# Small group's sums in 128x32 strips behind the low-rank sums, and two edits in the first slot

## The chip, the cores and the metric

The kernel runs on one core of a Trainium2 chip. The metric is the device time of one execution in microseconds (us). Before the change it was 979.74 us, the median of three runs (979.51 to 979.88).

The engines' short names are PE (TensorE; PEld is its weight load), DVE (VectorE), ACT (ScalarE), POOL (GpSimd) and SP (SyncE, which here issues nearly all DMAs).

## The reference

There are eight batches of 3136 rows and 256 columns; z has 64 columns, the low rank is 32, the hidden width 1024. Attention without softmax comes first, then a mixer over rows of low rank, then a two-layer mixer over columns:

```python
scores = (1 / S) * z @ z.T
attn = maximum(scores, 0) ** 2
x = u * (attn @ v)                       # B x 3136 x 256
h = x.T @ U @ V                          # U: 3136 x 32, V: 32 x 3136
u2 = x + h.T
out = u2 + maximum(u2 @ w_ch1, 0) @ w_ch2
```

## The kernel before

**Tiles.** 3136 rows are 24 tiles of 128 and one of 64. They are worked on in seven groups per batch: six of 512 rows (g = 0 to 5) and the *small group* (g = 6, 64 rows). Time goes in 56 *slots*, t = 7 b + g. A slot of g < 6 runs the attention stream of its group, `av_stream`: 48 steps in each of two "ways" of two 64x128 matmuls each, on the upper and the lower half of the rows, that run at the same time and write to different PSUM banks. `pair` (L174 to L184) issues two such matmuls. Seven slots later comes the group's low-rank part (`u2_unit`), and eight slots later its two-layer mixer (`ch1_part`, `ch2_stream`).

**Order.** Everything is emitted in a hand-written order into each engine's queue, which runs strictly in that order. In `emit` a slot has a list of light units (the streams) and queues of items (place, need, turn, function): an item is issued ahead of the light unit whose number is its place, if `need` of the four PSUM tiles are free by the planner's books, or else up to 14 units later. An item of need 0 is never put off. An item with `turn` first puts a no-op on POOL that waits for PE (`post`), changes the way of the attention stream and, in the first slot, takes one entry of `spare`: two casts of a piece of v on POOL (`cast_v`, L1310). The planner's clock counts one unit for a pair of matmuls of 256 columns. `hold(due, f)` runs `f` when that clock has reached `due`, or earlier when something that is emitted needs it. `book` keeps what each of ACT, DVE and SP is thought to be busy until.

**Scores.** A score pair (512 columns in two banks) must be rectified and squared. `rectify` with `whole` in the first slot chooses by the books among three ways: `both` (ACT rectifies, DVE squares later), `act` (two passes of ACT) and `dve` (`one_pass`: DVE rectifies and squares at once). The list `ways` gives the first choices by hand; with it empty, the way that ends first is taken. The first slot has fifteen such calls: one ahead of it, then at places 4, 16, 24, 30, 40, 46, 50, 56, 64, 68 (the pair called "last"), 72, 78, 84 and 88.

**First slot.** `cast_tail` (place 58) casts z's and v's last 64 rows, `z_turn` at place 62 transposes z's on PE (L331). The casts of v's six pieces are on POOL: one piece before the slot and one with each of the turns at places 4, 12, 24, 40 and 56.

**Sums of the small group.** Its attention output (64 rows) is `av_small`: 52 matmuls in the 64x64 form, four at a time, which end as four partial sums in two banks and two halves of the partitions. `four_sums` adds them: ACT copies the upper half (L759), DVE adds the lower half (L761), DVE adds the two banks (L763). `ch2_small` does the same for its second mixer layer (16 matmuls, L1145). For batches 2 to 7 both run one after the other in slot g = 0 at place 72: `ch2_small` of batch b - 2 and `av_small` of batch b. For batches 0 and 1 `av_small` runs alone, and for batches 6 and 7 `ch2_small` runs alone at the end.

**Low-rank sums.** `t1_all` (x.T @ U, L825 and L835) runs in 128x32 *strips*: all 128 rows, four column strips with different tiles of the sum, four matmuls at a time. It runs in slot g = 0 of the batch after (place 8), and for the last batch in the last slot. Its upper half is added to the lower by ACT (L847), DVE (L848) and a DVE copy (L849); `u2_unit` (L910) of the same slot needs it. The sixth piece of v of batch b (the last 512 full rows) is cast in slot g = 6 of the batch before or at the start of slot g = 0, by the function `cast`, which takes ACT or DVE, whichever is free first by the books (L204, L206).

Of the kernel before, what the change touches and what calls it, by code (L numbers as in the profile page):

```python
# [18 lines left out]
def kernel(  # L19
# [11 lines left out]
    nc = tc.nc  # L31
# [73 lines left out]
    ways = ["both", "dve"]  # L105
# [198 lines left out]
    def load_u(b, g):  # L304
        g0, gw = groups[g]
        if gw >= P:
            t = pool.tile([P, GT, D], FP32, name="u_sb", bufs=2)
            nc.sync.dma_start(
                out=t[:, : gw // P, :],
                in_=rows_of(u[b])[:, g0 // P : (g0 + gw) // P, :],  # L310
            )
        else:
            t = pool.tile([P, 3, D], FP32, name="u_small", bufs=1)
            nc.sync.dma_start(out=t[:gw, 0, :], in_=u[b, g0 : g0 + gw, :])
        queued(gw)
        u_sbs[b, g] = t
# [49 lines left out]
    def rectify(dst, src, b, part=1, whole=False):  # L366
# [24 lines left out]
        return book("act", ready, 8.7 if part == 1 else 5.3), None  # L391
# [335 lines left out]
    def av_small(b, g):  # L727
        k, ps = take_ps()
        rows = groups[g][1]
        xs[b, g] = pool.tile([P, 1, D], BF16, name="x_small")  # L730
        nc.vector.memset(xs[b, g][rows:, 0, :], 0.0)
        for jt in range(NQ + 1):
            while (b, jt) not in v_cast:
                run_held(min(h[0] for h in held))
        for jt in range(NT + 1):
            c = jt % 2
            part = slice(0, D) if jt < NF else slice(c * D // 2, (c + 1) * D // 2)
            at = min(jt, NF)
            for h in range(2):
                nc.tensor.matmul(  # L740
                    out=ps[c * hp : c * hp + rows, h, part],
                    lhsT=smalls[b][h * hp : (h + 1) * hp, place_of(at), :],
                    rhs=v_bfs[b][h * hp : (h + 1) * hp, at, part],
                    start=(jt < 2),
                    stop=(jt >= NF),
                    tile_position=(h * hp, c * hp),
                )
        pe(NT / 2 + 2)
        u1 = u_sbs[b, g]
        four_sums(k, ps, u1[:rows, 1:3, :])  # L750
        nc.vector.tensor_tensor(
            out=xs[b, g][:rows, 0, :], in0=u1[:rows, 1, :], in1=u1[:rows, 0, :], op=ALU.mult
        )
        book("dve", clock[0] + 3, 3)

    def four_sums(k, ps, t):

        rows = t.shape[0]
        nc.scalar.copy(out=t, in_=ps[hp : hp + rows, :, :D])  # L759
        ready = book("act", clock[0] + 3, 5)  # L760
        nc.vector.tensor_tensor(out=t, in0=ps[:rows, :, :D], in1=t, op=ALU.add)  # L761
        ps_free[k] = book("dve", ready + 1, 6)
        nc.vector.tensor_tensor(out=t[:, 0, :], in0=t[:, 0, :], in1=t[:, 1, :], op=ALU.add)  # L763
        book("dve", ready, 4)
# [53 lines left out]
    def t1_all(b):  # L818
# [26 lines left out]
        up = pool.tile([P, D], FP32, name="t1_up", bufs=1)  # L845
# [15 lines left out]
    def u2_unit(b, g, turn=True):  # L861
# [145 lines left out]
    def small_relu(b, g):  # L1007

        return flat_of(relus[b, g][0])[:, : NH * groups[g][1]]

    def ch1_small(b, g, way, box):
# [4 lines left out]
        if way == 0:  # L1016
            relus[b, g] = [take_block()]
# [106 lines left out]
    def ch2_out(b, g, acc):  # L1124

        for e in relus.pop((b, g)):
            give_block(e)
# [10 lines left out]

    def ch2_small(b, g):
        k, ps = take_ps()  # L1140
        rows = groups[g][1]
        for kt in range(NH):
            c = kt % 2
            for h in range(2):
                nc.tensor.matmul(  # L1145
                    out=ps[c * hp : c * hp + rows, h, :D],
                    lhsT=small_relu(b, g)[h * hp : (h + 1) * hp, kt * rows : (kt + 1) * rows],
                    rhs=w2_bf[h * hp : (h + 1) * hp, kt, :],
                    start=(kt < 2),
                    stop=(kt >= NH - 2),  # L1150
                    tile_position=(h * hp, c * hp),
                )
        pe(NH / 2 + 2)
        sums = u2s[b, g][:rows, 1:3, :]
        four_sums(k, ps, sums)
        ch2_out(b, g, sums[:, 0:1, :])
        book("dve", clock[0] + 3, 3)
# [156 lines left out]
    def cast_tail():  # L1314
        t0, n, entry, raw = zraw[2]
        for c in range(2):
            on_dve(out=z_bfs[0][:, NF, c, :], in_=raw[:, 2 * GT * dqk : n * dqk])
        v_tail(0, n, raw, on_dve)
        book("dve", clock[0], 5)
# [75 lines left out]
    for t in range(n_items):  # L1395
# [11 lines left out]
        if t > NG and g_now == NQ and b_next < B:  # L1407
            hold(clock[0] + 60 + 70, lambda b=b_next: load_u(b, NQ))
# [58 lines left out]
        elif av:  # L1467
# [20 lines left out]
        else:  # L1488

            small = (lambda: None) if early(*att) else (lambda: av_small(*att))  # L1490
            order = mine[:1] + [small] + mine[1:]
            if mix:
# [6 lines left out]
                else:  # L1499
                    order = up + [small, c0, c1, d0, d1, c2, c3, lambda: t1_all(att[0]), d2, d3]  # L1500
# [82 lines left out]
```

## Time and profile before

| what | us |
|---|---|
| median of three runs | 979.74 |
| the profiled execution | 979.08 |
| its span (first to last instruction) | 977.30 |
| PE busy | 969.4 |
| DVE busy | 633.7 |
| ACT busy | 480.0 |
| POOL busy | 15.7 |
| ps<-attn_small sums, L740, 8 batches, busy | 13.7 |
| ps<-relu sums, L1145, 8 batches, busy | 5.0 |
| ps<-x sums, L825 and L835, 8 batches, busy | 8.3 |
| last matmul's end | 973.02 |

The times of the prediction are microseconds from the span's start. A timeline line has start, duration, engine, line and operation, the tiles written and read, the array form of a matmul (64*128 and so on), and how often it is repeated; in brackets stand the engine's idle time ahead of it and what ended that. Matmuls overlap: one of 256 columns takes 0.27 us from its start to its end, so what counts is from start to start.

### The profile page before, as it was taken

To read this page: it belongs to the slowest core of one execution; us is meant where nothing else is said; L and a number is where in the kernel's file an instruction comes from. 1 tells how busy PE (TensorE), PEld (TensorE's weight loads), DVE (VectorE), ACT (ScalarE), POOL (GpSimd) and SP (SyncE) were. 2 spreads that over 40 slices of the span, in tenths; PEclk is the share of its full clock that TensorE was granted. 3 is DMA by queue.
4 is the path that set the end of the run, shared out by engine and by line. 5 is a ranking of instruction groups with operands and counts; after the bars stand their busy time and mean duration, and the time that the engine had idled before them with its cause. 6 is when DMAs were issued, how large, how long until landed. Compare 5 with 4: busy or idle time off the path is not lost.

```text
span 977.3 us, 35450 instructions
## 1 busy us (share of the span) xinstructions
PE 969.4 (99%) x16211; PEld 774.7 (79%) x16211; DVE 633.7 (65%) x815; ACT 480.0 (49%) x562; POOL 15.7 (2%) x25
## 2 busy tenths in 40 slices
PE   8999999999999999999999999999999999999998
PEld 6798777887778777787778877788777888778765
DVE  6887865668556775557756577556765667653363
ACT  8877732457334563345543365433653346531353
POOL 4200000000000000000000000000000000000000
PEclk9999999999999999999999999999999999999999
DMA  9999899989988799997999679996999968974142
GB/s 271 193 202 223 207 208 209 201 192 182 198 211 161 182 197 189 210 147 186 182 222 195 139 185 198 213 185 131 198 213 202 192 133 183 179 137 101 50 116 98
DMA packets 372549, 176.37 MB, mean 180 GB/s; under 512 B 347312, under 2 KB 350896, under 8 KB 372400
## 3 DMA queue, kind: packets, MB, share of 16 engines
q1 hardware_dynamic: 372256, 173.98, 87.2%
q8 instruction: 126, 2.06, 0.9%
q14 instruction: 23, 0.19, 0.1%
q10 hardware_dynamic: 144, 0.13, 0.0%
HBM read 62.56 MB, written 25.69 MB: 90 GB/s over the span
## 4 chain that ended last, share of the span: by engine, by line
PE 98%; DVE 1%; ACT 0%; issue 0%; DVEq 0%
PE ps L184 95%; PE ps L740 1%; PE ps L825 1%; PE ps L1145 0%; ACT blk L390 0%; DVE blk L364 0%; PE ps L1349 0%; PE ps L331 0%; DVE blk L553 0%; DVE blk L397 0%; DVE x_bf L775 0%; ACT last_sb L390 0%; DVE blk L1113 0%; PE ps L542 0%; DVE blk L761 0%
## 5 line engine op out<-in xcount | busy, mean ns | idle before, releaser
L184 PEld LDWEIGHTS <-blk 64*128 64x128 bf16 x12288 | 610.9, 94 | 152.6 <-POOLq L174 8.9
L184 PE MATMUL ps<-v_bf,blk 64*128 64x256 bf16 x9216 | 610.2, 269 | 1.0 <-DVE blk L364 0.8
L390 ACT ACTIVATE blk<-ps 128x1024 bf16<-128x1024 f32 (+1 forms) x335 | 313.8, 969 | 344.0 <-PE ps L184 339.0
L364 DVE TENSOR_TENSOR blk<-blk 128x1024 bf16<-128x1024 bf16 x350 | 222.3, 658 | 46.2 <-ACT blk L390 45.6
L184 PE MATMUL ps<-u2T,w_bf 64*128 64x512 bf16 (+1 forms) x1792 | 226.2, 349 | 0.0
L1002 DVE TENSOR_SCALAR blk<-ps 128x1024 bf16<-128x1024 f32 x111 | 135.9, 1224 | 103.7 <-PE ps L184 102.8
L184 PE MATMUL ps<-w_bf,blk 64*128 64x256 bf16 x3072 | 189.8, 269 | 0.0
L1005 ACT ACTIVATE blk<-ps 128x1024 bf16<-128x1024 f32 x81 | 82.2, 1022 | 123.9 <-PE ps L184 120.1
L184 PE MATMUL ps<-zzT 64*128 64x512 bf16 (+2 forms) x898 | 128.1, 326 | 0.6 <-ACT zzT L340 0.6
L184 PEld LDWEIGHTS <-w_bf 64*128 64x128 bf16 x1792 | 82.2, 94 | 27.9 <-POOLq L174 5.2
L775 DVE TENSOR_TENSOR x_bf<-ps,u_sb 128x1024 bf16<-128x1024 f32 x48 | 58.7, 1222 | 68.4 <-PE ps L184 68.4
L910 DVE TENSOR_TENSOR out_sb<-ps,x_bf 128x1024 f32<-128x1024 f32 x42 | 51.4, 1223 | 57.4 <-PE ps L184 57.4
L1131 DVE TENSOR_TENSOR out_sb<-ps,out_sb 128x1024 f32<-128x1024 f32 x42 | 51.4, 1224 | 19.2 <-PE ps L184 19.2
L184 PEld LDWEIGHTS <-zzT 64*128 64x128 bf16 x898 | 41.6, 94 | 6.3 <-ACT zzT L340 0.8
L206 DVE CAST v_bf<-stage 128x1024 bf16<-128x1024 f32 (+1 forms) x35 | 21.5, 615 | 0.0
L386 DVE TENSOR_SCALAR blk<-ps 128x1024 bf16<-128x1024 f32 x14 | 17.1, 1223 | 6.5 <-PE ps L184 5.8
L184 PE MATMUL ps<-t_sb,V_bf 64*128 64x256 bf16 (+1 forms) x208 | 20.3, 265 | 0.0
L204 ACT CAST x_bf<-out_sb 128x1024 bf16<-128x1024 f32 x19 | 19.7, 1037 | 0.0
L184 PE MATMUL ps<-v_bf,last_sb 64*128 64x256 bf16 x192 | 18.5, 269 | 0.0
L1131 DVE TENSOR_TENSOR blk<-ps,blk 128x1024 f32<-128x1024 f32 x5 | 6.1, 1225 | 11.9 <-PE ps L184 11.8
L204 ACT CAST v_bf<-stage 128x1024 bf16<-128x1024 f32 x13 | 13.5, 1040 | 0.0
L626 ACT ACTIVATE attn_small<-ps 128x512 bf16<-128x512 f32 (+1 forms) x32 | 13.1, 499 | 0.0
(86 smaller groups left out, 239.1 us busy)
## 6 DMA issues: line engine op xcount, KB each, us to landing
u_sb<-in_u_dram SPq DMA_DIRECT2D x48, 512.0 KB, 5.1
stage<-in_v_dram SPq DMA_DIRECT2D x42, 512.0 KB, 6.4
out_dram<-out_sb SPq DMA_DIRECT2D x42, 512.0 KB, 3.1
stage<-in_z_dram SPq DMA_DIRECT2D x7, 512.0 KB, 6.3
blk<-in_v_dram SPq DMA_DIRECT2D x5, 512.0 KB, 6.1
out_dram<-blk SPq DMA_DIRECT2D x5, 512.0 KB, 2.8
blk<-blk SPq DMA_TRANSPOSE x156, 5.1
blk<-in_moe_w_ch_dram SPq DMA_DIRECT2D x4, 512.0 KB, 5.5
```

The source lines that it names most:

```text
L184: ins = nc.tensor.matmul(**args)
L204: nc.scalar.copy(out=out, in_=in_)
L206: nc.vector.tensor_copy(out=out, in_=in_)
L364: nc.vector.tensor_tensor(out=a, in0=a, in1=a, op=ALU.mult)
L386: nc.vector.tensor_scalar(out=dst, in0=src, scalar1=scale, scalar2=0.0, op0=ALU.mult, op1=ALU.max)
L390: nc.scalar.activation(out=dst, in_=src, func=AF.Relu, scale=scale)
L626: nc.scalar.activation(out=dst[:, jj], in_=src[:, jj], func=AF.Relu, scale=scale)
L775: nc.vector.tensor_tensor(out=xs[b, g][:rows, :n, :], in0=four(box["ps"])[:rows, :n, :], in1=u_sbs[b, g][:rows, :n, :], op=ALU.mult,)
L910: nc.vector.tensor_tensor(out=o, in0=four(ps), in1=x, op=ALU.add)
L1002: nc.vector.tensor_single_scalar(out=r, in_=ps[:, :, :gw], scalar=0.0, op=ALU.max)
L1005: nc.scalar.activation(out=r, in_=ps[:, :, :gw], func=AF.Relu)
L1131: nc.vector.tensor_tensor(out=o, in0=acc, in1=o, op=ALU.add)
```

## The change

1. `av_small` and `ch2_small` become `small_sums`, whose matmuls are 128x32 strips (`in_strips`): per tile of the sum two matmuls of 128 rows by 32 columns instead of two of 64 by 64, and even and odd tiles of the sum in different halves of the partitions. So two partial sums are left instead of four; ch2's go to bank 0 and the attention's to bank 1 of one PSUM tile, one ACT copy and one DVE add serve both.
2. It is called right behind `t1_all` (`both_sums`) at place 8 of slot g = 0 for batches 2 to 7, with a need of two PSUM tiles. The ch2 part there is that of batch b - 3 (from batch 3 on), one batch later than before; batch 5's comes in the last slot behind `t1_all`. In the last phase batch 7's moves from place 9 to place 5. u2's place becomes 12 instead of 22 there.
3. The buffers follow: the small group's u2 in `out_small`, its relu in `relu_small` (no block of the shared store), t1's scratch and the sums' in `out_sb`; the small group's u is loaded 10 instead of 130 units into slot g = 6.
4. In the first slot `ways` gives ten choices: the sixth and the tenth call are `dve` too. In the books a rectify on ACT counts 9.3 instead of 8.7 in the first two slots.
5. `cast_tail` casts on POOL, and books nothing on DVE.

```diff
-    ways = ["both", "dve"]
+    ways = ["both", "dve", "both", "both", "both", "dve", "both", "both", "both", "dve"]
...
-            ends = {"dve": dve + DVE, "act": act + 19, "both": max(act + 8.7, dve) + 7.5}
+            ends = {"dve": dve + DVE, "act": act + 19, "both": max(act + 9.3, dve) + 7.5}
...
-        return book("act", ready, 8.7 if part == 1 else 5.3), None
+        return book("act", ready, 5.3 if part != 1 else 9.3 if slot[0] < 2 else 8.7), None
...
+    def in_strips(ps, bank, lhs, rhs, n, odd):
+        m = P // NREP
+        for i in range(n):
+            whole = i < n - 1 or not odd
+            for c in range(NREP) if not whole else (i % 2 * 2, i % 2 * 2 + 1):
+                w = c % 2
+                part = slice(0, D) if whole else slice(c // 2 * D // 2, (c // 2 + 1) * D // 2)
+                nc.tensor.matmul(
+                    out=ps[c * m : (c + 1) * m, bank, part],
+                    lhsT=lhs(i, slice(w * m, (w + 1) * m)),
+                    rhs=rhs(i)[:, part],
+                    start=(i < 2),
+                    stop=(i >= n - 2 if not odd else not whole),
+                    tile_position=(0, c * m),
+                )
+        pe(n / 2 + 1)
+
+    def small_sums(second, first, into=None):
+        k, ps = take_ps()
+        rows = groups[NQ][1]
+        if second is not None:
+            in_strips(
+                ps, 0,
+                lambda i, w: small_relu(second, NQ)[:, i * rows : (i + 1) * rows][:, w],
+                lambda i: w2_bf[:, i, :],
+                NH, False,
+            )
+        if first is not None:
+            b = first
+            xs[b, NQ] = pool.tile([P, 1, D], BF16, name="x_small")
+            nc.vector.memset(xs[b, NQ][rows:, 0, :], 0.0)
+            for jt in range(NQ + 1):
+                while (b, jt) not in v_cast:
+                    run_held(min(h[0] for h in held))
+            in_strips(
+                ps, 1,
+                lambda i, w: smalls[b][:, place_of(i), w],
+                lambda i: v_bfs[b][:, i, :],
+                NT, True,
+            )
+        at, end = 0 if second is not None else 1, 2 if first is not None else 1
+        n = end - at
+        t = (into or sums_tile())[:rows]
+        nc.scalar.copy(out=t[:, at:end], in_=ps[hp : hp + rows, at:end, :D])
+        ready = book("act", clock[0] + 3, 1 + 2 * n)
+        nc.vector.tensor_tensor(out=t[:, at:end], in0=ps[:rows, at:end, :D], in1=t[:, at:end], op=ALU.add)
+        ps_free[k] = book("dve", ready + 1, 1 + 2.5 * n)
+        if first is not None:
+            nc.vector.tensor_tensor(
+                out=xs[first, NQ][:rows, 0, :], in0=t[:, 1, :], in1=u_sbs[first, NQ][:rows, 0, :], op=ALU.mult
+            )
+            book("dve", clock[0] + 3, 3)
+        if second is not None:
+            ch2_out(second, NQ, t[:, 0:1, :])
+            book("dve", clock[0] + 3, 3)
...
+    def sums_tile():
+        return pool.tile([P, GT, D], FP32, name="out_sb", bufs=3)
+
+    def both_sums(b, second, first):
+        t = sums_tile()
+        t1_all(b, t)
+        small_sums(second, first, t)
...
+        elif n < GT:
+            o = pool.tile([P, 1, D], FP32, name="out_small", bufs=2)
...
-            relus[b, g] = [take_block()]
+            relus[b, g] = pool.tile([P, NH * gw], BF16, name="relu_small", bufs=1)
...
-            on_dve(out=z_bfs[0][:, NF, c, :], in_=raw[:, 2 * GT * dqk : n * dqk])
-        v_tail(0, n, raw, on_dve)
-        book("dve", clock[0], 5)
+            on_pool(out=z_bfs[0][:, NF, c, :], in_=raw[:, 2 * GT * dqk : n * dqk])
+        v_tail(0, n, raw, on_pool)
...
-            hold(clock[0] + 60 + 70, lambda b=b_next: load_u(b, NQ))
+            hold(clock[0] + 10, lambda b=b_next: load_u(b, NQ))
...
-                qc.append((64, 2, False, lambda: av_small(1, NQ)))
-            if fin:
-                qc.append((72, 2, False, lambda: (ch2_small(*fin), av_small(att[0], NQ))))
+                qc.append((64, 2, False, lambda: small_sums(None, 1)))
...
-                    order = up + [small, c0, c1, d0, d1, c2, c3, lambda: t1_all(att[0]), d2, d3]
+                    order = up + [small, c0, c1, d0, d1, c2, c3, lambda: both_sums(att[0], B - 3, None), d2, d3]
...
-                qm.append((8, 1, False, lambda: t1_all(u2i[0])))
-            qm.append((22 if u2i[1] == 0 else 40, 1, False, lambda: u2_unit(*u2i)))
+                sums = t > NG
+                b = att[0]
+                qm.append(
+                    (8, 2 if sums else 1, False,
+                        lambda: both_sums(b - 1, b - 3 if b > 2 else None, b) if sums else t1_all(b - 1))
+                )
+            qm.append((40 if u2i[1] else 12 if sums else 22, 1, False, lambda: u2_unit(*u2i)))
...
-                qm.append((9, 1, False, lambda b=B - 2 if k == 1 else B - 1: ch2_small(b, NQ)))
+                qm.append((9 if k == 1 else 5, 1, False, lambda b=B - 2 if k == 1 else B - 1: small_sums(b, None)))
```

More of the change, by code (lines that the diff above doesn't have):

```diff
@@ L312, in load_u @@
         else:
-            t = pool.tile([P, 3, D], FP32, name="u_small", bufs=1)
+            t = pool.tile([P, 1, D], FP32, name="u_small", bufs=1)
             nc.sync.dma_start(out=t[:gw, 0, :], in_=u[b, g0 : g0 + gw, :])
@@ L723, in av_stream @@
         return Ways(2 * NF, 1, step, box)
-    def av_small(b, g):
-        k, ps = take_ps()
[L729 to L764, printed above, removed]
+    def in_strips(ps, bank, lhs, rhs, n, odd):
[14 more added lines that the diff above has]
+        pe(n / 2 + 1)
@@ L843, in t1_all @@
         pe(7)
-        up = pool.tile([P, D], FP32, name="t1_up", bufs=1)
+        up = (into or sums_tile())[:, 2, :]
         t1 = pool.tile([P, D], BF16, name="t1_sb")
@@ L1136, in ch2_out @@
             give_block(o_blocks.pop((b, g)))
[L1139 to L1157, printed above, removed]
     def emit(light, queues, av=None, slack=14, hurry=14):
```

26 lines of the change are left out of this document (21 added, 5 removed).

## The prediction

> **What bounds the kernel now.** I read the page first: busy times, then the chain that ended last.
>
> ```profile
> PE 969.4 (99%) x16211; PEld 774.7 (79%) x16211; DVE 633.7 (65%) x815; ACT 480.0 (49%) x562; POOL 15.7 (2%) x25
> ...
> PE 98%; DVE 1%; ACT 0%; issue 0%; DVEq 0%
> ```
>
> TensorE is the chain. Since a busy PE need not be at its peak, I took the busy time by stretches (engine order PE, PEld, DVE, ACT, POOL):
>
> ```profile
> 4.80:27.00 22.20, 19.56 (x278) 12.63 (x279) 18.29 (x27) 19.38 (x23) 9.90 (x14) 1.00 1.03 288
> 27.00:930.00 903.00, 903.00 (x15260) 729.42 (x15256) 589.50 (x757) 437.78 (x514) 5.14 (x5) 1.00 0.91 182
> ```
>
> From 27 us on PE never idles, at a granted clock of 1.00. Only in the first slot are ScalarE (19.4 of 22.2 us) and VectorE (18.3) nearly full, and PE waits. So the change can act in three places: work or pauses of PE itself, the first 27 us, and the end. A steady pair of 64x128 matmuls over 256 columns starts every 0.109 us (eight pairs from 333.53 to 334.41 below); a four of 128x32 or 64x64 matmuls also takes 0.11 (24 of L825 in 0.66 us). Then I looked, in the PE timeline of one batch, at what surrounds the two groups that the change joins:
>
> ```profile
> 331.86 0.93 PE L184 MATMUL ps<-v_bf,blk 64*128 64x256 bf16 x14
> 332.73 0.84 PE L825 MATMUL ps<-x_bf,U_bf 128*32 128x256 bf16 x24
> 333.39 0.20 PE L835 MATMUL ps<-x_small,U_bf 128*32 128x64 bf16 x4
> 333.53 1.05 PE L184 MATMUL ps<-v_bf,blk 64*128 64x256 bf16 x16
> 334.41 0.49 PE L184 MATMUL ps<-zzT 64*128 64x256 bf16 x4
> ...
> 341.41 1.36 PE L184 MATMUL ps<-v_bf,blk 64*128 64x256 bf16 x22
> 342.70 0.63 PE L1145 MATMUL ps<-w_bf,blk 64*64 64x256 bf16 x16
> 343.17 1.54 PE L740 MATMUL ps<-v_bf,attn_small 64*64 64x256 bf16 x52
> 344.63 1.05 PE L184 MATMUL ps<-v_bf,blk 64*128 64x256 bf16 x16
> ```
>
> 331.86 to 334.41 is 2.55 us. Fifteen pairs (1.64), six fours (0.65) and a four of 64 columns (0.03) make 2.32: a visit to the 128x32 form loses 0.23 us going in and out. 341.41 to 344.63 is 3.22; eleven pairs (1.20), sixteen fours (1.74) and one of 128 columns (0.06) make 3.00: 0.22, and 0.01 more in the pair behind. From 342.70 to 343.17, where L1145 gives way to L740 in one form, four fours take 0.47, hardly over 0.44. So the loss belongs to a change of the array's form.
>
> **Part 1, the merge.** The matmuls stay: per batch 16 for ch2 and 52 for the attention sums, four at a time before and after, 0.11 us a four in either form. What goes are visits. Before: 8 of t1, one each of the attention sums alone (batches 0 and 1), 6 joint ones, and ch2 alone for batches 6 and 7 at the end: 18. After: attention 0, t1 0, attention 1, then t1+sums for slots 14, 21, 28, 35, 42 and 49, t1+ch2 in the last slot, and the two at the end: 12. Six fewer by 0.23: **-1.4 us**.
>
> The ACT copy (0.58) and VectorE add (0.68) that the two sums now share, and the second adds (0.42 each) that strips don't need, hang on engines with slack; I cost their loss at nothing. Loading u_small 120 clock units sooner puts one 64 KB transfer (5.5 us to land) some 9 us ahead of its use, and moves it on SP's queue ahead of the small turn (326.79), which is needed by 337. The small out-DMA moves to the first third of the slot; what then stands behind it on SP is the turn of x_bf (339.15), at worst 1 us later, and its reader runs after 344. Again nothing.
>
> It adds one wait. The attention sums, formerly at 343.17, now follow t1 and so need the last piece of v, whose cast is put on ACT just behind t1's copy:
>
> ```profile
> 333.65 0.37 ACT L847 COPY t_up<-ps 64x256 f32<-64x256 f32 x1 [0.55 <-PE ps L835]
> 333.92 1.04 ACT L204 CAST v_bf<-stage 128x1024 bf16<-128x1024 f32 x1
> 334.99 1.51 ACT L390 ACTIVATE blk<-ps 128x512 bf16<-128x512 f32 x2
> ```
>
> The cast ends 1.57 us after L835 starts (334.96 - 333.39), and with 0.06 for the signal PE may read it at 1.63. PE arrives at that piece (the eleventh four) after 0.03 + 0.44 for ch2 + 1.09 = 1.56: it waits 0.07, in five batches; in slot 14 there is no ch2 ahead and it waits 0.5. Together **+0.8**, between 0 (a free VectorE takes the cast) and 2 (0.3 each of ACT lateness). All queued behind that matmul on PE waits with it. VectorE meanwhile stands at the sums' add until ACT's copy, about 336.6, so L910 of the same slot ends near 339.2 instead of 338.4; its reader, the turn, has the slack above. t1's scratch (t_up) moves into the three out_sb buffers, in the place that the small group's output held in their turn: nothing.
>
> **Part 2, the first slot.** What PE waits for there:
>
> ```profile
> 16.15 0.69 DVE L364 TENSOR_TENSOR blk<-blk 128x1024 bf16<-128x1024 bf16 x1 [1.20 <-ACT blk L390]
> ...
> 17.69 1.23 POOL L1310 CAST v_bf<-blk 128x512 bf16<-128x512 f32 x2 [1.50 <-PE ps L184]
> 17.70 0.71 DVE L1317 CAST z_bf<-blk 128x64 bf16<-128x64 f32 x2
> ...
> 18.47 0.23 PE L331 MATMUL ps<-ident,z_bf 128*128 128x128 bf16 x1
> ...
> 26.77 0.28 PE L184 MATMUL ps<-v_bf,blk 64*128 64x256 bf16 x2 [0.85 <-DVE blk L364]
> ```
>
> (a) The sixth pair (place 40, score 14.67) goes to VectorE: 15.09 plus 1.26 (pass L397 to square, 7.63 to 8.89), so its square starts at 16.35, not 16.15. PE, which waited for that square until 16.90, resumes at 17.10: +0.2.
> (b) The tails. GpSimd's two casts of v's last piece are queued at place 56 behind a wait for PE, the tail casts at place 58. They start when those end, 18.92 + 0.2 = 19.12. GpSimd's cast of 64 columns isn't in the trace: its 512-column casts take 0.61, a 256-column one 0.40, its 128x1 memsets 0.10. I take 0.25, on the line of the two casts; ends 0.10 and 0.40. Two of them end at 19.62, and L331, in order on PE, starts at 19.65 instead of 18.47: **+1.2** (0.9 to 1.5). This is no relief but a transfer to the later queue.
> (c) What VectorE gains: 1.4 us of tail casts (17.70 to 19.07) leave it, so the square that held PE from 19.40 to 19.72 is in time: -0.2; the "last" pair is issued one unit sooner: -0.1. Its score: 20.06 to 20.9.
> (d) After the ten given ways the planner chooses. Following its bookings by hand (L364 to L400, two one-pass pairs of 18.2 on VectorE): VectorE booked to 186.8 when the "last" pair comes, ACT only to 166.1, so "last" goes to ACT twice (189 against 194.3), then both, VectorE, ACT twice, VectorE. ACT keeps five passes behind "last", as now. With ACT starts 0.93 apart, VectorE 1.26 + 0.65 a pair: the last pair's score at 24.35, its square at 26.81, PE resumes at 27.56 (square start + 0.75, as 26.03 to 26.77), against 26.77.
> So the first slot costs **+0.8**, between -0.2 (tails free) and +1.5 (0.40 each and one more wait for PSUM). From there PE is full as before.
>
> GpSimd and VectorE also slow each other here: VectorE squares of 0.69 took up to 1.09 beside GpSimd's casts (9.73). The Trainium skill, SBUF — State Buffer, "Who interferes with whom", goes further: a VectorE instruction with two SBUF inputs and a GpSimd instruction that reads SBUF exclude each other for a whole instruction. By that rule the three tail casts (0.25, 0.25, 0.40) would hold back up to 0.9 us of squares; by the row up to 0.4. In the order above VectorE has no square between 18.7 and 21.7, so the sum is the same by either.
>
> **Part 3, the end.** The last sums move from place 9 to 5 (0.44 us) and lose 0.9 us of chain, so VectorE is free when the last halves are done: its L1113 follow PE's end at 973.02 by 0.05 instead of 973.18: **-0.1**.
>
> **Sum.** -1.4 + 0.8 + 0.8 - 0.1 = +0.1 on the profiled execution's 979.08 us (span 977.30 and 1.78 around it): 979.2. The median of the three runs lies 0.66 above that execution: **979.8 us**. About 0.2% (1.96 us: 977.78 to 981.70) is what a measurement can tell from no change.
>
> **Rivals.**
> The relief works: no wait for the tails, and the waits of 0.2, 0.2 and 1.0 (26.77) go. For it: both engines near full, and the chain that ended last runs through ACT's passes from 20.48. Against it: GpSimd's queue order. -1.4 + 0.8 - 1.4 - 0.1 = -2.1: 977.6. Chance 0.16, two thirds of it beyond 0.2%.
> Slot 1 starves for PSUM: with VectorE's last squares first, x_bf follows the last square (26.81 + 0.65 + 1.22) and ends near 28.7 instead of 26.1 and holds its tile 2.6 us longer. It decides if a score pair is forced before then: one pair's pass of 1.0 and a square of 0.7 lost: +1.7 more, 981.5. For it: only four tiles; against it: the planner delays pairs rather than force them. Chance 0.13, a third beyond 0.2%.
> The sums wait for the whole v tile, not its last piece: 1.63 - 0.47 = 1.16 in five batches, 1.6 in one: 7.4 in place of 0.8, 986.4. Against it: PE ran v matmuls from 333.53 on while that cast was under way. Chance 0.05.
> Weights of strips aren't hidden: L825's loads take 97 ns each; 17 fours in each of 8 batches would pay 13 us: 993. Against it: L825's fours run at 0.11 us with four such loads inside. Chance 0.02. The Trainium skill, TensorE: Matmul & The Clock Gate, "The mechanism", says that loads overlap matmuls only if their row groups differ, and all strips use the same rows; L825's row contradicts it.
> The sum as worked out has 0.64.
>
> **Numbers.** Faster by over 0.2%: 0.11; slower: 0.04 + 0.05 + 0.02, with a little for what I haven't seen, 0.13; within: 0.76. The range reaches to the first two rivals: 977.8 to 981.8.
>
> **What would show it.** Right: twelve visits to small forms; in each merged one a PE wait under 0.1 us on ACT L204 (0.5 in slot 14); L331's last matmul near 19.65 waiting for POOL; PE's full stretch starting near 27.6. Wrong: a GpSimd tail cast before 18.5, or PE resuming before 26.5; idle PE in slots 1 or 2; over 0.5 us of wait per batch at the attention strips.

## The result and the profile after

| us | before | after |
|---|---|---|
| median of six runs each | 979.93 (979.51 to 981.09) | 984.10 (983.82 to 986.15) |
| ratio | | 1.0045, 95% interval 1.0035 to 1.0055 |
| the profiled execution | 979.08 | 984.12 |
| its span | 977.30 | 982.34 |
| last matmul's end to the end of the span | 4.28 | 3.69 |

The change costs 4.2 us; 979.8 was forecast, with a range up to 981.8. The page after, engines and chain:

```profile
PE 969.3 (99%) x16211; PEld 783.3 (80%) x16211; DVE 624.6 (64%) x793; ACT 475.2 (48%) x555; POOL 16.6 (2%) x28
...
PE 93%; DVE 2%; DMA 2%; ACT 1%; SPq 1%; issue 0%; POOL 0%; DVEq 0%; ACTq 0%
```

TensorE has the same number of matmuls and the same busy time, and 5 us more of span: the loss is idle time of PE. The chain that ended last was 98% PE before; now it passes through VectorE, a DMA and SyncE's queue. The busy time by stretches (PE, PEld, DVE, ACT, POOL, then granted clock, DMA share and GB/s) says where PE idles:

```profile
4.80:27.00 22.20, 18.32 (x262) 12.29 (x261) 17.90 (x23) 16.94 (x21) 11.10 (x17) 1.00 0.97 283
27.00:46.00 19.00, 17.25 (x268) 13.15 (x264) 17.04 (x23) 14.99 (x17) 4.63 (x5) 1.00 0.74 145
46.00:930.00 884.00, 882.57 (x14924) 722.33 (x14919) 563.12 (x717) 418.05 (x492) 0.00 (x0) 1.00 0.91 182
```

Before, the second of these rows was

```profile
27.00:46.00 19.00, 19.00 (x306) 14.88 (x302) 17.22 (x24) 16.67 (x18) 5.14 (x5) 1.00 0.88 179
```

and in the third, too, PE was busy for the whole 884.00 us. So the waits are in the first slot, *in the slot behind it*, and in few places later. VectorE and ScalarE do no more work in the first two rows than before: they are not fuller, they are late.

Setting the same instruction of both traces side by side gives the balance. Profiled executions differ ahead of the sixth score pair (its score starts at 14.67 before), also where the first slot is the same program: by -0.09, 0.23, 1.60 and 1.69 us in four with the changed one. So here and in the experiments the lateness of that instruction is subtracted for what happens in the first two slots.

| up to | after is late by | gained since |
|---|---|---|
| the sixth pair's score (14.67 before) | -0.09 | |
| batch 0's score corner, L615 (74.10) | 3.20 | +3.29 |
| batch 2's score corner (195.10) | 4.11 | +0.91 |
| t1 in the last slot (922.53) | 3.31 | -0.80 |
| the last matmul's end (973.02) | 5.62 | +2.31 |
| the end of the span (977.30) | 5.04 | -0.58 |

**First slot and the one behind it.** The waits of PE, from its timeline:

```profile
17.34 0.61 PE L184 MATMUL ps<-v_bf,blk 64*128 64x256 bf16 x8 [0.57 <-DVE blk L364]
20.06 0.23 PE L331 MATMUL ps<-ident,z_bf 128*128 128x128 bf16 x1 [1.16 <-POOL z_bf L1332]
23.48 0.61 PE L184 MATMUL ps<-v_bf,blk 64*128 64x256 bf16 x8 [0.18 <-DVE blk L364]
29.53 1.10 PE L184 MATMUL ps<-v_bf,blk 64*128 64x256 bf16 x14 [1.06 <-DVE blk L364]
...
35.33 0.28 PE L184 MATMUL ps<-v_bf,blk 64*128 64x256 bf16 x2 [0.34 <-DVE blk L364]
45.15 0.39 PE L184 MATMUL ps<-zzT 64*128 64x512 bf16 x2 [0.32 <-DVE x_bf L798]
```

From start to start, less the matmuls' own time, these are 0.73, 1.33, 0.35, 1.24, 0.50 and 0.50 us; with the smaller ones (0.24 at 24.82, 0.15 at 30.14, 0.19 at 39.74) they make 5.2, and all waits of before in the same places make 1.9. The first two are in the prediction; those from 23.48 on are not, and the wait for the last pair's square, which it keeps, is gone. On VectorE at 29.53:

```profile
27.05 0.69 DVE L364 TENSOR_TENSOR blk<-blk 128x1024 bf16<-128x1024 bf16 x1
27.66 1.22 DVE L798 TENSOR_TENSOR x_bf<-ps,u_sb 128x1024 bf16<-128x1024 f32 x1
28.79 1.28 DVE L364 TENSOR_TENSOR blk<-blk 128x1024 bf16<-128x1024 bf16 x2
32.00 1.54 DVE L364 TENSOR_TENSOR blk<-blk 128x1024 bf16<-128x1024 bf16 x1 [1.92 <-ACT blk L390]
```

and before:

```profile
24.89 1.22 DVE L775 TENSOR_TENSOR x_bf<-ps,u_sb 128x1024 bf16<-128x1024 f32 x1
26.03 1.28 DVE L364 TENSOR_TENSOR blk<-blk 128x1024 bf16<-128x1024 bf16 x2
```

The square that PE waits for (28.79) had its input from ScalarE at 27.68, and stood behind x_bf. The order of the two is that of before, 2.8 us later. Then VectorE idles 1.92 us before 32.00, because ScalarE waits for PE's next scores: one late step goes round the three engines.

**Last slot.** SyncE's queue before, then SyncE's queue and PE after:

```profile
922.02 1.18 SPq L811 DMA_TRANSPOSE u2T<-x_small  x1
```

```profile
928.11 0.52 SPq L1168 DMA_DIRECT2D out_dram<-out_small  x1
928.73 1.19 SPq L834 DMA_TRANSPOSE u2T<-x_small  x1
```

```profile
931.12 0.41 PE L184 MATMUL ps<-u2T,w_bf 64*128 64x64 bf16 x16 [1.72 <-DMA u2T<-x_small]
```

The turn of x_small (the DMA that transposes it for PE) now stands behind the small out-DMA of batch 5. That DMA waits for the small sums' last add on VectorE (L1166, 927.66 to 928.08), so PE gets u2T 1.9 us late. The turn had no slack to lose: before, it landed at 925.43, 3.4 us after its issue, and PE read it at 925.49.

**The merge.** The joined groups of one batch, and ScalarE beside them:

```profile
335.82 1.26 PE L184 MATMUL ps<-v_bf,blk 64*128 64x256 bf16 x20
337.01 0.84 PE L856 MATMUL ps<-x_bf,U_bf 128*32 128x256 bf16 x24
337.67 0.20 PE L866 MATMUL ps<-x_small,U_bf 128*32 128x64 bf16 x4
337.70 0.61 PE L735 MATMUL ps<-w_bf,relu_small 128*32 128x256 bf16 x16
338.14 1.62 PE L735 MATMUL ps<-v_bf,attn_small 128*32 128x256 bf16 x52
339.69 0.28 PE L184 MATMUL ps<-v_bf,blk 64*128 64x256 bf16 x2
```

```profile
338.20 1.04 ACT L204 CAST v_bf<-stage 128x1024 bf16<-128x1024 f32 x1
```

Ten pairs end 1.09 us after 335.82; the way into the form takes 0.10 more. From L856 to the next pair of L184 are 2.68 us: 22 fours of 0.109 and two short ones (0.03 and 0.06) make 2.49, the wait for the cast that ends at 339.24 is 0.07, and 0.12 is the way out. A batch takes 119.35 us here and took 119.50 before.

### The profile page after: what moved, and what is told of

Its sections match the earlier page's. It is cut to its first block, busy times and chain, and to the rows that moved or that the text cites. A ratio compares the mean times of both kernels' runs of the same rounds, so it can differ in the third digit from the quotient of the medians.

```text
span 982.3 us, 35422 instructions
## 1 busy us (share of the span) xinstructions
PE 969.3 (99%) x16211; PEld 783.3 (80%) x16211; DVE 624.6 (64%) x793; ACT 475.2 (48%) x555; POOL 16.6 (2%) x28
## 4 chain that ended last, share of the span: by engine, by line
PE 93%; DVE 2%; DMA 2%; ACT 1%; SPq 1%; issue 0%; POOL 0%; DVEq 0%; ACTq 0%
PE ps L184 91%; PE ps L735 1%; DVE blk L364 1%; DMA blk<-in_v_dram 1%; PE ps L856 1%; DMA stage<-in_z_dram 0%; DVE blk L397 0%; SPq L220 0%; ACT blk L390 0%; DMA stage<-in_v_dram 0%; DVE blk L1035 0%; DVE x_bf L798 0%; DMA u2T<-x_small 0%; DVE blk L386 0%; SPq L1337 0%
## 5 line engine op out<-in xcount | busy, mean ns | idle before, releaser
L184 PEld LDWEIGHTS <-blk 64*128 64x128 bf16 x12288 | 619.5, 94 | 148.0 <-POOLq L174 8.9
L184 PE MATMUL ps<-v_bf,blk 64*128 64x256 bf16 x9216 | 610.6, 269 | 3.2 <-DVE blk L364 2.2
L390 ACT ACTIVATE blk<-ps 128x1024 bf16<-128x1024 f32 (+1 forms) x330 | 310.0, 966 | 351.8 <-PE ps L184 334.7
L364 DVE TENSOR_TENSOR blk<-blk 128x1024 bf16<-128x1024 bf16 (+1 forms) x349 | 220.5, 658 | 50.0 <-ACT blk L390 49.4
L184 PE MATMUL ps<-u2T,w_bf 64*128 64x512 bf16 (+1 forms) x1792 | 226.8, 349 | 1.7 <-DMA u2T<-x_small 1.7
L1035 DVE TENSOR_SCALAR blk<-ps 128x1024 bf16<-128x1024 f32 x111 | 135.9, 1224 | 112.8 <-PE ps L184 112.8
L184 PE MATMUL ps<-w_bf,blk 64*128 64x256 bf16 x3072 | 190.0, 269 | 0.3 <-DVE blk L1035 0.3
L184 PE MATMUL ps<-zzT 64*128 64x512 bf16 (+2 forms) x898 | 129.0, 326 | 0.6 <-DVE x_bf L798 0.3
L184 PEld LDWEIGHTS <-w_bf 64*128 64x128 bf16 x1792 | 83.1, 94 | 29.1 <-POOLq L174 5.1
L798 DVE TENSOR_TENSOR x_bf<-ps,u_sb 128x1024 bf16<-128x1024 f32 x48 | 58.8, 1224 | 68.4 <-PE ps L184 67.7
L1166 DVE TENSOR_TENSOR out_sb<-ps,out_sb 128x1024 f32<-128x1024 f32 x42 | 51.4, 1224 | 19.2 <-PE ps L184 19.2
L184 PEld LDWEIGHTS <-zzT 64*128 64x128 bf16 x898 | 42.9, 94 | 6.3 <-issue 1.7
L184 PE MATMUL ps<-t_sb,V_bf 64*128 64x256 bf16 (+1 forms) x208 | 20.3, 265 | 0.0
L184 PE MATMUL ps<-v_bf,last_sb 64*128 64x256 bf16 x192 | 18.6, 269 | 0.0
L1166 DVE TENSOR_TENSOR blk<-ps,blk 128x1024 f32<-128x1024 f32 x5 | 6.1, 1225 | 12.5 <-PE ps L184 12.4
L735 PE MATMUL ps<-v_bf,attn_small 128*32 128x256 bf16 (+1 forms) x416 | 12.9, 269 | 0.3 <-ACT v_bf L204 0.3
```

Source lines behind the costliest of these rows:

```text
L184: ins = nc.tensor.matmul(**args)
L364: nc.vector.tensor_tensor(out=a, in0=a, in1=a, op=ALU.mult)
L390: nc.scalar.activation(out=dst, in_=src, func=AF.Relu, scale=scale)
L735: nc.tensor.matmul(out=ps[c * m : (c + 1) * m, bank, part], lhsT=lhs(i, slice(w * m, (w + 1) * m)), rhs=rhs(i)[:, part], start=(i < 2), st ...
L798: nc.vector.tensor_tensor(out=xs[b, g][:rows, :n, :], in0=four(box["ps"])[:rows, :n, :], in1=u_sbs[b, g][:rows, :n, :], op=ALU.mult,)
L1035: nc.vector.tensor_single_scalar(out=r, in_=ps[:, :, :gw], scalar=0.0, op=ALU.max)
```

## The experiments

Kernels that ran together shared runs of the kernel before, whose medians were 980.3 to 980.5; each ratio is to those runs (it need not be the quotient of the two medians). "Late" means late against the trace of the kernel before. Two theories stood at first. Mine: all later waits come of the first slot's lateness, carried on by the planner's changed books. The rival: each place has its own cause.

**1. The merge alone** (`merge_only`): the ways, the bookings of 9.3 and the casts of the tails as before.

```
-    ways = ["both", "dve", "both", "both", "both", "dve", "both", "both", "both", "dve"]
+    ways = ["both", "dve"]
...
-            ends = {..., "both": max(act + 9.3, dve) + 7.5}
+            ends = {..., "both": max(act + 8.7, dve) + 7.5}
...
-            on_pool(out=z_bfs[0][:, NF, c, :], in_=raw[:, 2 * GT * dqk : n * dqk])
+            on_dve(out=z_bfs[0][:, NF, c, :], in_=raw[:, 2 * GT * dqk : n * dqk])
```

> The change with the two edits of the first slot undone (ways, 9.3 and the tail casts as before), so only the joint sums and their buffers and places. Theory: the first slot's edits cost what the first seventy microseconds show (the first L615 at 77.49 us instead of 74.28, +3.2) and also the two waits at 100.70 and 129.22 (0.33 and 0.52), which come of the later state of the queues. Then L615 is back near 74.3, the joint sums save six visits (-1.4) and cost the wait for v's last piece (+0.84), the last slot's wait for the small turn stays (+1.9), the end is 0.6 shorter: about +0.7 against the kernel before, 980.7 us. Rival: the waits at 100.70 and 129.22 belong to the joint sums' buffers; then they are here too and the kernel is at +1.6, 981.5 us. Second rival: the joint sums cost most of the loss by themselves; then 983 or more.

Measured: 981.48, ratio 1.0013 (1.0004 to 1.0022). The first slot costs nothing (lateness 0.34 at the sixth pair and at 74.10), but the 1.0 us in slots 7 and 8 is there, without any lateness of the first slot:

```profile
97.84 0.39 PE L184 MATMUL ps<-zzT 64*128 64x512 bf16 x2 [0.17 <-DVE t_sb L879]
126.45 0.61 PE L184 MATMUL ps<-w_bf,blk 64*128 64x256 bf16 x8 [0.34 <-DVE blk L1035]
```

So is the wait in the last slot. My theory of one cause falls: these two belong to the merge.

**2. The first slot alone** (`slot_only`): the kernel before, with the ways, the 9.3 and the tails on POOL, without their booking of 5 on VectorE.

```
-    ways = ["both", "dve"]
+    ways = ["both", "dve", "both", "both", "both", "dve", "both", "both", "both", "dve"]
...
-            on_dve(out=z_bfs[0][:, NF, c, :], in_=raw[:, 2 * GT * dqk : n * dqk])
+            on_pool(out=z_bfs[0][:, NF, c, :], in_=raw[:, 2 * GT * dqk : n * dqk])
```

> The kernel before with the first slot's edits alone (ten given ways, 9.3, the tails on POOL). Theory: +3.2 us at the first L615, and 0.9 more by slot 8 if those waits follow from the first slot: 983.1 to 984.0 us. Rival: the first slot's loss needs the joint sums: under 981.

Measured: 984.08, ratio 1.0032 (1.0019 to 1.0044). The lateness grows from 1.69 at the sixth pair to 4.76 at 74.10, by 3.07, with the waits of after (1.24, 0.50, 0.19 and 0.50 in the slot behind), and stays at 4.75 or 4.76 up to 922.53. The first slot's cost is its own and causes nothing up to the last slot. There this trace loses another 0.6, though its sums are the old ones and the queue has the old order:

```profile
930.83 0.41 PE L184 MATMUL ps<-u2T,w_bf 64*128 64x64 bf16 x16 [0.42 <-DMA u2T<-x_small]
```

The turn of x_small takes 4.0 us to land here instead of 3.4. So it does in experiment 5 (4.1 us, a wait of 0.64), and in 6 it takes 3.7 (0.24). Why it is slower there, no run shows.

**3. The last slot's two DMAs turned round** (`turn_first`): the changed kernel, with what is held run ahead of `both_sums` in the last slot, so that the turn of x_small is issued first.

```
-    ... c2, c3, lambda: both_sums(att[0], B - 3, None), d2, d3]
+    ... c2, c3, lambda: (run_held(clock[0] + 40), both_sums(att[0], B - 3, None)), d2, d3]
```

> The change with one difference: in the last slot what is held is emitted ahead of the joint sums, so that on SP's queue the turn of batch 6's small group stands ahead of the out-DMA of batch 5's small sums. Nothing else moves. Theory: the 1.9 us that PE waits at 931.12 for the small turn are that DMA's wait for VectorE's last add (927.66 to 928.08) with the turn queued behind it; they go, 982.2 us. Rival: the turn is late for its own data or for the DMA rings; then under 0.5 us goes, 983.6 or more.

Measured: 982.48, ratio 1.0023 (1.0014 to 1.0032). The queue and PE in the last slot:

```profile
926.68 1.16 SPq L834 DMA_TRANSPOSE u2T<-x_small  x1
929.45 0.53 SPq L1168 DMA_DIRECT2D out_dram<-out_small  x1
```

```profile
930.59 0.40 PE L184 MATMUL ps<-u2T,w_bf 64*128 64x64 bf16 x16
```

No wait is left there: from t1 to the last matmul the kernel loses 0.42 instead of 2.31. Those 0.42 are batch 5's sixteen ch2 matmuls (0.44), which came into this slot, as batch 0's left slot 14.

**4. The tails on VectorE again** (`tails_dve`): the changed kernel, with `on_dve` for `on_pool` in `cast_tail`, and its booking of 5.

> The change with the tails of z and v cast by VectorE again, the ways and 9.3 left as changed. The planner then takes for the last five pairs ACT alone, both, both, VectorE, ACT alone instead of ACT alone, both, VectorE, ACT alone, VectorE. Theory: the wait of 1.3 us at the transposition of z's tail (20.06) is the tails' alone and the rest of the first slot's loss (some 1.9 us at the first L615) comes of the pairs on VectorE: L331 near 18.7, 984.1 - 1.3 = 982.8 us. Rival A: the tails are the whole loss: 981 us. Rival B: the wait is taken back at once by another, since ACT and VectorE are full: no change, 984.1.

Measured: 982.05, ratio 1.0016 (1.0007 to 1.0025). Sixth pair 1.12 late, at 74.10 2.00: the ways cost 0.88, and in the changed kernel (3.29) the move of the tails is worth 2.4 of the 3.3. L331, at 19.71, waits for nobody here.

**5. and 6. The ways alone and the tails alone** (`ways_only`, `tails_only`): the kernel before, each with its part of the diff of experiment 2.

> The kernel before with the ten given ways and 9.3, the tails on VectorE. The planner takes the same ways as in tails_dve. Theory: +0.9 us at the first L615, as in tails_dve, where it goes into the square of the sixth pair (PE to 17.3 instead of 16.9) and into the last pairs: 980.9. Rival: with VectorE at two more passes and the tails, over 2 us.

> The kernel before with the tails of z and v cast by POOL, nothing else. The first slot's ways are those of before. Theory: L331's wait at z's tail is 1.1 us longer (19.6 instead of 18.47), 0.2 comes back at the square that VectorE now has in time, and the rest is handed on: +1.0 us at the first L615, 981 us against 980. Rival A: the tails cost what tails_dve took off the change, 2.4 us: 982.4. Rival B: ACT and VectorE use the pause and the wait at 26.77 (1.01) shrinks by as much: no change.

Measured: 981.67, ratio 1.0010 (1.0001 to 1.0019), for the ways; 982.26, also 1.0010 (1.0001 to 1.0019), for the tails. From the sixth pair to 74.10 the ways lose 0.87 (1.52 to 2.39), the tails 1.51 (1.26 to 2.77). The tails' loss is the one wait of L331:

```profile
21.45 0.23 PE L331 MATMUL ps<-ident,z_bf 128*128 128x128 bf16 x1 [1.73 <-POOL z_bf L1317]
```

The tails' trace has two more waits, 0.49 in slot 8 (see experiment 9) and the 0.24 in the last slot. Alone, the two edits make 2.38 up to 74.10; together they cost 3.07. The 0.7 between is more than these figures scatter (0.3 at most: five kernels whose first slot is as before lose 0.00 to 0.28 there). It lies at the end of the first slot and in the slot behind: from the wait that answers to the one before 26.77 on, PE waits 1.33 in the kernel before, 1.34 with the tails, 1.79 with the ways, and 2.59 with both, of which 0.50, 0.19 and 0.50 are waits that neither brings alone (0.35 in their place with the ways).

**7. The square ahead of x_bf** (`x_second`): the changed kernel; only the first slot's x_bf (L798) is issued 18 clock units later.

```
-        if slot[0] < 2:
+        if slot[0] < 2 and (b, g) != (0, 0):
             run_held(clock[0] + 14)
...
-        av_out(b, g, box)
+        if (b, g) == (0, 0):
+            hold(clock[0] + 18, lambda: av_out(b, g, box))
+        else:
+            av_out(b, g, box)
```

> The changed kernel, with only the first slot's product x_bf (L798) issued 18 clock units later, so that on VectorE the square of the next slot's first pair stands ahead of it instead of behind it. My theory: of the 3.2 us that the first slot's edits cost, about 1.1 come of that square's standing behind x_bf (ACT's pass ends at 27.68, the square starts at 28.79), so TensorE's wait of 1.24 us before 29.53 shrinks to 0.1 to 0.2, and x_bf, which ends 0.6 us later, holds nobody. At the first matmul of the last halves of slot 0's successor (74 us) the kernel is 2.1 behind the one before instead of 3.2, and the time is about 983.0. Rival: VectorE has no room left there at all, so the wait goes to the next square and to the bank that x_bf holds 0.6 us longer: no gain, 984.1 or more.

Measured: 984.84, ratio 1.0046 (1.0034 to 1.0059): no gain. The wait before 29.53 is gone, and the next pair's square now stands behind x_bf:

```profile
27.16 1.36 DVE L364 TENSOR_TENSOR blk<-blk 128x1024 bf16<-128x1024 bf16 x2
28.43 1.22 DVE L798 TENSOR_TENSOR x_bf<-ps,u_sb 128x1024 bf16<-128x1024 f32 x1
29.57 0.68 DVE L364 TENSOR_TENSOR blk<-blk 128x1024 bf16<-128x1024 bf16 x1
```

```profile
30.30 0.50 PE L184 MATMUL ps<-v_bf,blk 64*128 64x256 bf16 x6 [1.12 <-DVE blk L364]
```

It is 1.29 us instead of 1.24, and the three waits behind it are the same to 0.01. The rival was right: x_bf's place in the queue only chooses which square is late. I read this as VectorE coming out of the first slot about one such pass too late, whatever stands first. Before, x_bf was done by 26.1, while PE waited for another square anyhow.

**8. The merge with the DMAs turned round** (`merge_turn`): experiments 1 and 3 together.

> As books, but with the changed bookings: the joint sums alone with the small turn first. Theory: 1.9 us under merge_only and 1.0 over books: at the kernel before, -0.2 to +0.1 us against it. Rival (the last slot's wait is taken by something else once the first slot is as before): as merge_only.

Measured: 979.72, ratio 0.9994 (0.9985 to 1.0003). The merge without its last slot's mistake gives back what it loses in slots 7 and 8 (0.96 in its trace).

**9. The old bookings** (`books`, and once more as `books_again`): experiment 8, with the books for the small sums as they were, though less work is now done.

```
-        ready = book("act", clock[0] + 3, 1 + 2 * n)
+        ready = book("act", clock[0] + 3, 5)
...
-        ps_free[k] = book("dve", ready + 1, 1 + 2.5 * n)
+        ps_free[k] = book("dve", ready + 1, 6)
+        book("dve", ready, 4)
```

> The joint sums alone (first slot as before), with the small turn ahead of the small out-DMA in the last slot, and with the planner's books for the small sums as before the change (5 on ACT, 6 and 4 on VectorE, where the change books 3 and 3.5 for a single sum). The order of ACT, VectorE and SP is then that of the kernel before up to slot 13. Theory: the waits of merge_only at 97.84 (0.33), 124.62 (0.15) and 126.45 (0.52) come of another order that the smaller bookings give slots 7 and 8; they go, and the joint sums show their own price: six visits less (-1.4), v's last piece +0.84, the end -0.6: 1.1 under the kernel before, 978.8 to 979.2 us. Rival: the waits belong to the buffers and stay: 980 us.

Measured: 978.97, ratio 0.9982 (0.9973 to 0.9991): faster than both kernels, by 0.2% against the one before. The second time it was 979.11, 0.9991 (0.9982 to 1.0000), hardly clear of it.

> The same kernel as books, beside the one with the earlier cast on the same chip: 979.0, 0.2% faster than the kernel before.

The traces show how a booking makes a wait. In the changed kernel SyncE's queue runs, in slots 7 and 8:

```profile
109.93 7.38 SPq L420 DMA_TRANSPOSE blk<-blk  x1
117.41 0.52 SPq L308 DMA_DIRECT2D u_sb<-in_u_dram  x1
117.98 0.42 SPq L256 DMA_DIRECT2D stage<-in_v_dram  x1
...
119.75 2.44 SPq L220 DMA_DIRECT2D stage<-in_z_dram  x2
```

and with the old bookings, as before:

```profile
110.89 0.33 SPq L308 DMA_DIRECT2D u_sb<-in_u_dram  x1
111.32 0.38 SPq L256 DMA_DIRECT2D stage<-in_v_dram  x1
111.75 5.24 SPq L420 DMA_TRANSPOSE blk<-blk  x1
...
118.35 2.07 SPq L220 DMA_DIRECT2D stage<-in_z_dram  x2
```

With smaller bookings the planner puts a turn (L420) ahead of two loads of 512 KB, and that turn stands 6.9 us for VectorE's L1035. The loads go out at 117.4, just ahead of z's and v's last rows, whose transfers take 5.4 and 3.7 us to land instead of 2.5 and 2.3 before. VectorE, whose next work is a cast of those rows, waits 2.18 us. In the kernel after:

```profile
125.88 0.75 DVE L206 CAST z_bf<-stage 128x576 bf16<-128x576 f32 x1 [2.18 <-DMA stage<-in_v_dram]
```

With the old bookings it waits 1.47 us there, before 1.30. L1035 is queued behind that cast, and PE waits 0.52 for it at 129.22. Experiment 9 differs from experiment 8 in nothing but books, and loses -0.02 and 0.31 there in its two traces, instead of 0.96. Of the wait at 97.84 (0.33, for t1's add L879) only that it goes with the books is shown: all six traces with the new bookings have it, none of the seven with the old ones.

The wait behind the cast is not the bookings' alone. The six have it with 0.27 to 0.52 us; of the seven, five don't have it, but experiment 9's second trace has 0.32 and experiment 6's, whose small sums are the old ones, 0.49. In these two the loads go out ahead of the turn, as before, but the last rows' transfers go out 0.4 and 0.6 us later than before, measured against PE, and the cast waits about 2 us. In experiment 6:

```profile
125.03 0.75 DVE L206 CAST z_bf<-stage 128x576 bf16<-128x576 f32 x1 [2.09 <-DMA stage<-in_z_dram]
```

So the new order makes this wait regular, and a queue that is late for another reason, which is not shown, can make it too.

**10. The cast of v's last piece earlier** (`early_v`): experiment 9, with that cast due 80 instead of 90 units into its slot, which puts it ahead of t1's copy on ScalarE.

```
-            hold(clock[0] + (90 if g_now == NQ and b_next > 1 else ...
+            hold(clock[0] + (80 if g_now == NQ and b_next > 1 else ...
```

> The fastest kernel so far (the merge alone, with the two DMAs of the last slot turned round and the old bookings), with the cast of v's last piece due 80 instead of 90 clock units into the slot, which puts it on ScalarE ahead of t1's copy instead of behind it. Theory: the attention strips' wait for that cast goes (0.07 us in five batches, 0.5 in slot 14), and t1's copy, 0.2 us later, delays nobody: 0.85 us less than that kernel, about 978.1. Rival: the planner, whose order changes with it, puts a wait of the same size elsewhere: 979.0.

Measured: 978.72, ratio 0.9981 (0.9972 to 0.9990), the fastest of all; beside it, on the same chip, experiment 9's kernel had 979.11. The strips no longer wait:

```profile
332.50 1.04 ACT L204 CAST v_bf<-stage 128x1024 bf16<-128x1024 f32 x1
333.56 0.37 ACT L879 COPY out_sb<-ps 64x256 f32<-64x256 f32 x1
```

```profile
333.25 0.61 PE L735 MATMUL ps<-w_bf,relu_small 128*32 128x256 bf16 x16
333.69 1.54 PE L735 MATMUL ps<-v_bf,attn_small 128*32 128x256 bf16 x52
335.16 0.28 PE L184 MATMUL ps<-v_bf,blk 64*128 64x256 bf16 x2
```

A batch gains 0.23 against the kernel before instead of 0.15, and slot 14's 0.50 is gone. From the sixth pair to the end the trace gains 1.8 us on the kernel before (0.14 late to 1.66 early); experiment 9's gained 0.4 in both its traces. Of those 1.4 between them, 0.85 are the waits for the cast; the rest lies in places that differ between traces of one kernel too (slots 7 and 8, and a wait of 0.26 before 223.48 in one of experiment 9's). The medians show 0.4, so the step's size rests on the traces.

## Why the prediction was wrong

**"Six fewer by 0.23: -1.4": right.** There are twelve visits instead of eighteen; a joined one loses 0.22 us in and out, so six make 1.3 (batches: 119.35 against 119.50, with a wait of 0.07 in each). That strips hide their weight loads was right too: PEld rises by 8.6 us and PE's pace doesn't change.

**"Together +0.8" for v's last piece: right**, 0.07 in five batches and 0.50 in slot 14, and experiment 10 takes them away.

**"So the first slot costs +0.8 ... From there PE is full as before": wrong; 3.29.** This is the step that failed first. Up to the pair where I stopped the number was near: L331 at 20.06 (19.65 forecast), and the matmul foreseen for 27.56 came at 27.86. The loss up to that point is 1.09, against the 0.8 of the text; of the surplus 0.2 is the sixth pair, whose square took 1.02 us behind a cast of POOL instead of 0.69 (PE waits 0.33 more than in experiments 2 and 7, and 0.12 of it comes back at L331). The way there was in part another, so that it came out near is in part luck: I let PE stand at that matmul for the last pair's square, as before at 26.77, and PE reached it without a wait, kept back instead at 23.48 and 24.82 (0.35 and 0.24). The step that failed is to stop there. The last pair's square is not the last thing that VectorE owes. Behind it stand x_bf and the squares of the next slot, and PE waits for them, or for a PSUM tile: 1.24, 0.50, 0.19 and 0.50 us against 0.32 before (two waits too short to show as idle time). That is the sign "idle PE in slots 1 or 2", which I had named. I had x_bf's late end (28.7 forecast, 28.88 measured) in a rival, asked there only for the PSUM tile that it holds, and not who is queued behind it. The tile did cost something, but for slot 1's product: the score at 45.15 waits 0.50 for slot 1's x_bf. By parts, the ways cost 0.87 where I had 0.2 for the sixth pair, the tails 1.51 where I had 1.2 less the 0.3 of (c), and both together 0.7 more. Which of the two edits' passes meet to make that 0.7 is not taken apart.

**"The small out-DMA moves to the first third of the slot ... Again nothing": right for slots g = 0, wrong for the last slot; 1.9 us.** I asked what stands behind that DMA only in the slot that I had looked at. In the last slot the order is written out by hand, and the turn that PE needs next is behind it; it had 0.06 us of slack before. Experiment 3 takes away the whole wait.

**"I cost their loss at nothing", of the copy and the adds that go: 0.9 us in slots 7 and 8.** The work itself costs nothing. But each goes with its booking, and the bookings decide the order of the queues: experiment 9 restores the books and nothing else, and 0.6 to 1.0 of the waits goes. The rest is at its edge in any case: 0.32 and 0.49 come with the old bookings too, in experiment 9's second trace and in experiment 6.

**"The end -0.1": right in kind, -0.6.** Before, VectorE was the chain there: three L1113 ran one after the other behind the small group's adds (L761, L763, L1131, until 972.66). I took the gap of the last matmul alone. All kernels with the merge end 3.7 us behind their last matmul, instead of 4.3.

The sum as the traces have it: +3.29 for the first slot and the one behind it, +0.91 for slots 7 and 8, +1.89 for the turn, -0.58 for the end, and -0.38 for the visits and the wait for v (-0.80 up to the last slot, of which 0.42 are matmuls that come back in it). With the -0.09 of the start this is 5.04 of span. The medians differ by 4.2, since the profiled execution of before was 0.85 quicker than its median.

**The rivals.** The relief did not come: PE waits longer for VectorE's squares, not shorter. (Its 977.6 lay just outside the range that was said to reach to it.) "Slot 1 starves" was right on where time is lost, not on why: PE waits there first for squares in VectorE's queue (1.24 and 0.50), and for PSUM tiles only later (0.19 at 39.74 for one that ScalarE reads, 0.50 at 45.15 for x_bf's). The whole v tile was not waited for, and no strip paid for its weights, against the rule of the Trainium skill's page TensorE: Matmul & The Clock Gate that the prediction cites: fours with equal row groups start 0.11 us apart (16 in 0.44 from 337.70).

## What to carry to other kernels

A stall that is moved is followed in each in-order queue until a wait is met that was there before; the pair after the last one that changes is part of the change. For a step that is emitted in several places, look at what stands behind it at each of them, the last above all, and at how long before its use each transfer lands. Where a planner orders the queues by estimates, an estimate is part of the program: when work goes, change the code and the books separately and look at each.

## What was not expected of the hardware

**The start.** PE's first matmuls run at half the pace for a time that varies from execution to execution. In the trace of experiment 2, and in that of after:

```profile
7.18 1.08 PE L184 MATMUL ps<-v_bf,blk 64*128 64x256 bf16 x8
8.46 1.30 PE L184 MATMUL ps<-v_bf,blk 64*128 64x256 bf16 x10
```

```profile
6.32 0.61 PE L184 MATMUL ps<-v_bf,blk 64*128 64x256 bf16 x8
7.09 1.07 PE L184 MATMUL ps<-v_bf,blk 64*128 64x256 bf16 x16
```

Pairs start 0.21 us apart in the one and 0.11 in the other, though the granted clock in the profile's rows is 1.00 in both stretches. In the first the slow pace holds until about 10 us, and the sixth pair is 1.69 us late behind it. Five of the thirteen traces are like this, those of experiments 2 to 6. All five have edits of the first slot, but so have after and experiment 7, which are not slow; after and experiment 3 run the same program up to the last slot. The Trainium skill, TensorE: Matmul & The Clock Gate, "What's actually happening", describes a clock at half rate until a window of some 3.4 us has been busy, a window that runs freely, so that the change comes at another time in each run. The factor of two agrees with it; the spread of some 3 us here is wider than the 500 ns either way that it gives. The row of the granted clock doesn't show it here.

It is not the only thing that varies: in the trace of experiment 8 the sixth pair is 1.44 us late with no slow pairs, since PE waits 1.10 us at 8.75. This is why a difference of one or two us between two single executions says nothing. Whether the medians of the kernel before (979.7 to 980.5) differ for the same reason is not shown.

**POOL beside VectorE.** A cast of 64 columns on POOL takes 0.23 us (the estimate was 0.25). The prediction says that POOL's casts and VectorE's squares slow each other; the traces show more exactly what happens. The one that starts first keeps its time, and the one that starts while it runs is longer by what the first had left, less 0.14 us. In the trace of after, the cast of 512 columns at 16.13 takes its 0.61, and the square that starts at 16.26, with 0.48 of it left, takes 1.02 instead of 0.69. The square at 17.92 takes its 0.69, and the cast that starts at 18.13, with 0.48 of it left, takes 0.95 instead of 0.61; L331 stands behind that cast. In the first slots of the thirteen traces 104 such squares and casts start while one of the other engine has 0.15 to 0.68 us left, and all follow this to 0.02 us. So the two shut each other out but for 0.14 us. A VectorE pass that reads PSUM (L397, at 15.00) does not: the cast that starts beside it at 15.57 takes 0.62, and the pass its 1.22.
